# A hand-ordered attention and feed-forward kernel: the later part of the order rewritten, 24 half tiles masked by GpSimd

## The chip, the core and the metric

The kernel runs on one core of a Trainium2 chip. The core has five engines that run side by side, each through its own instructions in order: TensorE (PE, and PEld for its weight loads) multiplies matrices into PSUM, VectorE (DVE), ScalarE (ACT) and GpSimd (POOL) work element by element, and SyncE (SP) issues transfers. The metric is the time of one execution on the device in microseconds (us); smaller is better. The kernel before takes 441.9 us, the median of three runs from 441.88 to 443.86 us.

## The reference

Eight batches of eight heads, 576 positions, 64 elements a head. Scores within `tau` of their row's maximum are kept; the others get no weight. What the attention returns goes through a feed-forward layer whose hidden units are the largest of three products.

```python
scores = scale * np.matmul(q, k.transpose(0, 1, 3, 2))
thresh = np.max(scores, axis=-1, keepdims=True) - tau
scores = np.where(scores >= thresh, scores, -1000000000.0)
scores = scores - np.max(scores, axis=-1, keepdims=True)
attn = np.exp(scores)
attn = attn / (np.sum(attn, axis=-1, keepdims=True) + 1e-09)
attn_out = np.matmul(attn, v)                     # (8, 8, 576, 64)
x = attn_out.transpose(0, 2, 1, 3).reshape(8 * 576, 512)
h = np.maximum(np.maximum(x @ w1, x @ w2), x @ w3)  # 512 -> 768
out = h @ w_out                                   # 768 -> 512
```

## The kernel before

The work is cut into **half tiles**: the scores of 128 query rows of one head against all 576 keys, 128x576 numbers in fp32. There are 36 of them in a batch and 288 in all; two make a step, whose normalised weights are turned by one transposing transfer. A "quad" is four heads of one batch. The last batch goes through the feed-forward layer in two parts (`SPLIT`), the others in one.

One half tile passes these stages, each written as one letter of the order:

- `S`: TensorE multiplies queries and keys into a PSUM bank `sc` (`scores`). Queries and keys were transposed before (`T`), copied out of PSUM (`a` on ScalarE into `qt`, `c` on VectorE into `kt`), and GpSimd copied the query halves across into `qs` (`q`).
- `m`: VectorE reads `sc`, writes the scaled, negated scores to a buffer `z` (or to `stage`, which served the weights earlier) and leaves the row's extreme value in `nm`.
- Then the mask and the exponential, in one of several ways that a digit of the table `MASKED` sets for each half tile. Digit 0: VectorE makes a threshold `th` out of `nm` (`s`, 128x1), ScalarE flattens what is below it (`e`, a Prelu with a tiny slope) and takes the exponential with a row sum into `sm` (`n`). Digit 1: ScalarE takes the exponential at once with `nm` as its bias (`e`), and VectorE zeroes what is too small and sums up (`k`, a SCALAR_TENSOR_TENSOR with `z` as both inputs). Digits 2 and 3 are these two with ScalarE reading the scores straight from PSUM.
- `r`: VectorE takes the reciprocal of a step's two sums (`rs`), `p`: GpSimd multiplies each half by it and writes `P` in bf16, `t`: SyncE starts the transfer that turns `P` into `ptq`.
- `O`: TensorE multiplies `ptq` by the values, `w` (VectorE) and `x` (ScalarE) copy the result to `xt`.

The feed-forward layer of a batch follows as soon as its attention is done, in pieces `F` with a second half `B`: `ph` for the three hidden products (copied by ScalarE, `h`, into `hm`; combined on VectorE, `v`, into `hm` and then `hT`), `po` for the output (copied by ScalarE, `u`, and stored, `o`). The rest of the letters are loads (`l`, `g`), casts on GpSimd (`y`, `z`), the ninth chunk of rows (`N`, `j`, `i`) and the end (`f`, `d`).

Nothing decides the order at build time: the string `ORDER` is the program, letter by letter, and a digit behind `S`, `T`, `O`, `F` or `N` names one of four PSUM slots. Every engine is wrapped in `_Ordered`, which makes each instruction follow the one before it on the same engine, so the letters of one engine are its queue. All instructions carry the line of that wrapper, L93, in the profile; they are told apart by their tiles' names. PSUM has the four slots and no more: TensorE can't start a piece before the slot's last reader is done.

Of the kernel before, what the change touches and what calls it, by code (L numbers as in the profile page):

```python
# [11 lines left out]
F32 = mybir.dt.float32  # L12
# [23 lines left out]
PBUFS = 6  # L36

SPLIT = {7: ((0, 1), (2, 3, 4))}

ORDER = """  # L40
lllllllllT0laqqlcT1aS2lcqqgmS0S3lemS1lmnT2lmeS3lsaS0mnqlqemT3lyerclcapsnS1lS2eqmlS3qemznmS2perS1mnpsmnpT3ske
ytS1erkpT2agmnT3pclesqS2aqetS0meqlrnspmS1eqsT2nmpS3tnrcS0zlemS2eprmS3npmtS0npsgS1sermpS2emyS3eptmT0eplmS1ayl
meS0kynS2tssT3snkynkercperlT3pmnpmntqremS0lasprgeT3pmeS2psstnplnS0mzecesqrmS3etqkeS2gpnmS1npsmtnS0prmleS3pmS
2npsmnS0yrsmetperS2epmO1eqtnkplemnzswT2teS3rplS1empnmS3tpnssrS1klepS0mapermtS2epmT1S3nmqtnkO2qemncpS3txrskT1
peS2rmeS0ptmegpamS2npS1ertsmpnlkzS2elmS3eS0mpnlO1srkepsmnO2tyeprgwnpmT1xS3cpeS0sszmF2eS1meBqkF0ngqT3shrsmBay
S2tvpnF3rpemS1BpemF0pnsvT2BnyctS1esrlsT2mphS3lezS1maF0myntpT2sS3ngrcqF1eBmpnS2svpBnrmS3peS0tmeyF2zmnF3lBsvep
S0rhkBptesF2mgeS1zvF0nsmBpteBsrgvpnF1kS3phS2semBnqmF0S3evqF2ntrmBpelS1spvBnlmS3qhF0rsmepS1tnBpsmS3ezvS2eS1rm
pF0etsyO3mnlkngpO2eswetkBxrmpT3nF2rvpaS1BnqmS0hspS3meF2prS1smntBzesmF3ezvT0tBeclT1yS2pnvS0apsmtS3eyrmlS1epS2
mepF0mnqsmnS3tkBnkeF1restpkumeS2prtBumlperkpS0ustS2umS3pesmS1eqtT0mO2nlpceqsrmO3ntywelkS0pxlS1meF3prnS2smBye
myF0thpskS1oeBpF2nlvF3nlrmBpeBkpS1hstsvS0eF3lrmpnF2mBepBsveF1nT0vBtarkS3lhqS2smleF0prF1mnBysntBveS2plvnS0pom  # L50
F3nyS1pmeBsysmF0thT2rrlpeS1clF3epsmBnqT2svBaS1evqS2nmF0pS3nmqBtnmT2pS1hrcpS3esmS0petF2melS1rmpBnF3skpetF0sve
BlBmnF2vhtF1esrBkpnS0vtT3npBmS2arvpS0ermO3eqtsmepT1swntpS0cF2epesmtnS3kT1nS0mtBessrkpameS3preS1mS0uqmuS3mpnS
1tsmS2pnoS0rempS3lempO1lnkqlemO2lnymeO0srkpetkeF3swxykxpT2BercnprtS1uyS2upmF0termqS3eBymN2lhsskpelkS0eF3ertm
S1pjBlmeS0plvF2npS1mnyF3tpmnBsopT0nvBaS1kF2ieqrssmS0hlpBmelT1qF3snrvF0epcBlepS2vBnpsmtS1nS3rmphS2mnpF1smeS0B
snmF3tevS2T0mF1atBrsekpBevS0thS2pmF3nymS1qeBrsmnpS0tvF2eplF1rmnpBskeBptF3hsvS0eBrsstpmnS1lvT2qeO0mpnlscnT3wS
1etF2srramS0lnqBmlF3eqvT1nBcpS0thF2pemS1perS3mpBnmS0ptesO1smpnkteF3yvxT0BraktyS2esS1vpeS0mpnS3meqF2mnyrmpnT0
S1lceBqmeptrskS0pulS3muS1epmS2teF0rmplnskpeS1mtO3eklekO2esrmpesBknpwxS1kutS2urmopS3nF0myeS1mBetpsmF2hlS3rkep
BlmnF0S1prnsvT3tepBmF2apsssvS1eBtqmeS0qrS3hmtS1epsmF2lnpF0mleF3koBnBrvpeBstyvS1phsS2nmF3emS0nrS1tpmBnprS2smn
F0pveF1pBsremT3ptevBpS2chF0tnmF3ekBT1nvS2aBsmlnF0qvS1eS2rtrespmS3eBmqF1hmpT2nBcpS3ekpT2O0sasvterlmpO2ekqntwS
3xklpS1eF2ssmnF0yrBnmyS3evBptemS1plhS2ssmT3eyF0rcpeF1mBpntT3vnByS2ravpS0nmtpS3nsmS1eF2srmpektepS3slmnS0Bmeqn  # L60
mT1ktuS3urS0lcpeO2rlmpelmpeO3klpelweF1kqnsxS0rkepS2tmS3eBymemepS0kuF3quT2smeBtrF1kphoS0aBmnpS3tsN2rnvplnmpS1
erkpF0tjsF3mnBpsseBvS2ihrS1pmelS0mqeF3S2mnytBpmnoS1rF0eprsvF2ntpmBeBvqF1htskpS3esS0rmetS2pnmF3pBnmF0pesvT2te
BcF1nsBrvpntBskphT2F3erS0vlapBmnF1qvS2etpBmT0hS3rscpnF2lmS1qesS0sempBemS3yF1nvtS0nmBnT2ssrmpO3etspveF0wnS1rk
BpaS3tmhS2elqsF1mlS0qnmS3ermpBF2espsmS0npvBeS3tmeS1rvpO0ntmnsmS2yxS3empF0eskyerT1mpeS2cBtnypsmelkS3ulS2muS1e
smT0O3nsrplnpO2awetmeF3rkpxseT0S1ycntS2meF0poBrnsmpnkpF1ukBurS2shBqemF3oepvS0lS2nsmqF1emBptBnvF0hrrS2speS3mp
F1emBpntT2vepF3BssaktS0nvlBemS2hS1rsmptF0nS3mpeBmtnT2F1svnF3cetBBsrnvpS2hsrqS0meS1pmeT3F2sprmaS0npBmeF3ptsvn
S1qS0mnBtqmeS2yF1prevS0epssBmnS3qmS2htpmF0nlF1keBsmBertvO3pnvepF0serwpT2nBcpF3hktS1eBsrsmpnT0S2vtpaS1remqT3S
0nmyF2qectT1BpasmS3epvS1nS0mqnF2rmpemtpT3eS1keqS0smBercntpS1mupS3emF0ukessS1rmtpnBmopkS2uskS1eO3rukekO0yxeO3
ynwtprmopS0xmpS2emF3peS1mteBrsmpS0nF2pmhtS1nkBS3evF0nstmN2erkpeF1mBjpsBevS2hskF0eF3rkpteBmF1nBpveBkO2hsrvpeS
0rtwS1pnmF2npmS3eBympF1ntrvS0epBmpS2rF3svtpeS0mnpS1sBmiF2smhF0ntkBBervpS1etF3smpnF2BervpS1hsBpnmF0tevS3F1nmB  # L70
etrBkpO2vhO3nspS1xrwepS0mpF3smS2etF1snmBeBstvnS2S0veS3meF1snkeF2rmpnmpeBnkBerrptukpuO3rN1xpuO0jpuO3wptF1xpF2
hF0tvF1vF3hF0vtF1vF2hF0viF1vF2ohF0voF1vF3hF2vF1vF3hF2vO1vO0wF2xF3F1huF0vF3vF2ohF1vF3vF2hF0vF1vF3hF0vF2vF3hF1
vF2vF0hF1vF2vF0uF1ouN0ofjdi
# [31 lines left out]
def kernel(  # L105
# [684 lines left out]
    x = 0  # L790
# [39 lines left out]
```

## Time and profile before

| | |
|---|---|
| median of the runs | 441.9 us |
| span of the profiled execution | 440.2 us |
| PE busy | 418.9 us, 95% |
| PEld busy | 313.6 us, 71% |
| ACT busy | 403.6 us, 92% |
| DVE busy | 393.9 us, 89% |
| POOL busy | 317.0 us, 72% |
| mean granted TensorE clock | 0.988 |

The profile gives the profiled execution's time by its span, 440.2 us from the first to the last instruction; the runs' times are 1.7 us or more above it. In 40 slices of the span the page shows the busy tenths: TensorE is at 9 from the seventh slice or so to the last but one, VectorE and ScalarE drop in the last three, GpSimd in the last eight.

### The profile page before, as it was taken

How to read it: one execution, taken by the hardware profiler on the slowest of the kernel's cores; microseconds unless marked ns; L12 is line 12 of the kernel's file. 1: busy time of each engine (PE TensorE's matmuls, PEld its weight loads, DVE VectorE, ACT ScalarE, POOL GpSimd, SP SyncE). 2: the span in 40 equal slices, each digit the busy share in tenths (PEclk: the TensorE clock that was granted, in tenths of full speed). 3: DMA queues.
4: the chain of work that ended last, by engine and by line, in shares of the span. 5: the costliest groups of instructions: out<-in, count | busy, mean ns of one | idle time of the engine just before them, and what ended most of it. 6: DMA issues, size and time to landing. Idle time of an engine off the chain costs nothing.

```text
span 440.2 us, 14283 instructions
## 1 busy us (share of the span) xinstructions
PE 418.9 (95%) x5188; PEld 313.6 (71%) x5190; DVE 393.9 (89%) x1248; ACT 403.6 (92%) x834; POOL 317.0 (72%) x420
## 2 busy tenths in 40 slices
PE   7696789999999999999999999999999999999996
PEld 6353446787788776787678777887688777786873
DVE  4888899999999999999999999999889999998542
ACT  4999999999999999999999999999999998989521
POOL 1988999998787778867786778886585776554400
PEclk9987999999999999999999999999999999999999
DMA  6999999999999999999999999999698778583812
GB/s 190 276 239 214 270 215 260 263 252 252 220 277 224 237 165 242 291 160 232 189 242 238 202 182 273 192 199 208 135 237 153 147 109 185 102 169 72 192 50 85
DMA packets 213959, 88.50 MB, mean 201 GB/s; under 512 B 189184, under 2 KB 202240, under 8 KB 213888
## 3 DMA queue, kind: packets, MB, share of 16 engines
q1 hardware_dynamic: 213360, 86.96, 95.4%
q8 instruction: 41, 0.67, 0.6%
q10 hardware_dynamic: 528, 0.62, 0.5%
q14 instruction: 30, 0.25, 0.2%
HBM read 35.65 MB, written 9.44 MB: 102 GB/s over the span
## 4 chain that ended last, share of the span: by engine, by line
PE 78%; DVE 5%; POOL 5%; issue 4%; ACT 3%; DMA 2%; SPq 1%; DVEq 0%; POOLq 0%; ACTq 0%
PE ph L93 31%; PE sc L93 26%; PE po L93 10%; PE o L93 8%; POOL P L93 4%; PE tp L93 3%; ACT z L93 3%; DVE z L93 3%; DMA qm<-in_q_dram 2%; SPq L93 1%; DVE kt L93 1%; POOL w L93 1%; DVE stage L93 0%; DVE hm L93 0%; POOL qs L93 0%
## 5 line engine op out<-in xcount | busy, mean ns | idle before, releaser
L93 POOL TENSOR_SCALAR P<-z,rs 128x576 bf16<-128x576 f32 x250 | 202.0, 819 | 59.1 <-DVE rs L93 30.4
L93 DVE TENSOR_SCALAR_CACHE_REDUCE z<-sc 128x576 f32<-128x576 f32 x250 | 183.2, 749 | 12.2 <-PE sc L93 8.1
L93 PE MATMUL sc<-kt,qs 64*128 64x256 f32 (+2 forms) x640 | 179.8, 417 | 5.5 <-DVE z L93 3.9
L93 PE MATMUL sc<-kt,qt 64*128 64x320 f32 (+2 forms) x640 | 180.9, 429 | 3.1 <-DVE z L93 1.2
L93 PE MATMUL ph<-xt,w 64*128 64x288 bf16 (+2 forms) x2160 | 172.0, 283 | 0.2 <-DVE hm L93 0.2
L93 PEld LDWEIGHTS <-w 64*128 64x128 bf16 (+1 forms) x2160 | 128.0, 94 | 31.6 <-issue 4.0
L93 ACT ACTIVATE z<-z,th 128x576 f32<-128x576 f32 x161 | 120.5, 767 | 2.2 <-DVE th L93 1.9
L93 ACT ACTIVATE z<-z 128x576 f32<-128x576 f32 x175 | 117.6, 674 | 0.2
L93 PEld LDWEIGHTS sc<-kt,qs 64*128 64x128 f32 (+1 forms) x640 | 92.4, 179 | 22.5 <-DVE z L93 8.6
L93 PEld LDWEIGHTS sc<-kt,qt 64*128 64x128 f32 (+1 forms) x640 | 92.0, 179 | 14.7 <-DVE z L93 3.5
L93 DVE SCALAR_TENSOR_TENSOR z<-z 128x576 f32<-128x576 f32 x75 | 61.7, 827 | 1.4 <-ACT z L93 1.1
L93 POOL COPY qs<-qt 64x640 f32<-64x640 f32 (+3 forms) x66 | 45.9, 695 | 19.5 <-ACT qt L93 16.1
L93 ACT ACTIVATE z<-z,nm 128x576 f32<-128x576 f32 x72 | 53.9, 767 | 0.0
L93 PE MATMUL po<-wo,hT 64*128 64x512 bf16 (+3 forms) x454 | 53.3, 354 | 0.3
L93 DVE TENSOR_TENSOR hm<-ph,hm 128x576 bf16<-128x576 f32 (+2 forms) x54 | 37.0, 685 | 9.8 <-PE ph L93 9.6
L93 ACT ACTIVATE hm<-ph 128x576 bf16<-128x576 f32 (+2 forms) x54 | 31.9, 590 | 14.3 <-PE ph L93 13.8
L93 PEld LDWEIGHTS <-hT 64*128 64x128 bf16 (+2 forms) x456 | 28.4, 95 | 18.5 <-issue 2.6
L93 DVE TENSOR_TENSOR hT<-ph,hm 128x576 bf16<-128x576 f32 (+2 forms) x54 | 36.9, 683 | 2.8 <-PE ph L93 1.0
L93 PE MATMUL o<-ptq,vb 128*64 128x512 bf16 (+2 forms) x544 | 38.7, 282 | 0.2 <-DVE z L93 0.2
L93 POOL TENSOR_SCALAR P<-stage,rs 128x576 bf16<-128x576 f32 x38 | 29.5, 783 | 11.7 <-DVE rs L93 8.4
L93 ACT ACTIVATION_READ_ACCUMULATOR z<-z 128x1 f32 x175 | 33.6, 192 | 0.0
L93 PEld LDWEIGHTS <-vb 128*64 128x64 bf16 x544 | 22.4, 111 | 14.0 <-issue 5.6
(44 smaller groups left out, 412.2 us busy)
## 6 DMA issues: line engine op xcount, KB each, us to landing
vm<-in_v_dram SPq DMA_DIRECT2D x32, 256.0 KB, 4.6
qm<-in_q_dram SPq DMA_DIRECT2D x15, 512.0 KB, 4.7
km<-in_k_dram SPq DMA_DIRECT2D x15, 512.0 KB, 5.4
out_dram<-ob SPq DMA_DIRECT2D x14, 512.0 KB, 4.5
stage<-in_moe_w_dram SPq DMA_DIRECT2D x9, 512.0 KB, 5.6
ptq<-P SPq DMA_TRANSPOSE x144, 4.5
vr<-in_v_dram SPq DMA_DIRECT2D x16, 128.0 KB, 3.8
stage<-in_moe_w_out_dram SPq DMA_DIRECT2D x3, 512.0 KB, 5.5
```

Of the source, the lines that this page charges most:

```text
L93: ins = fn(*a, **kw)
```

## The change

The change has two parts. First, the table `MASKED` differs from the fourth batch on: digits 4 and 5 are new. Digit 0 stands 189 times instead of 187, digit 1 59 times instead of 84, digit 2 14 times as before, digit 3 once instead of three times, digit 4 24 times, digit 5 once. The 24 stand in batches four to eight: 3, 4, 5, 6 and 6. Second, the later part of `ORDER` is written anew. On each engine the instructions stand as before until the work of the third batch's feed-forward layer and of the fourth batch's scores; from there on they are in another order.

A half tile with digit 4 takes this way: `m` and `s` on VectorE as with digit 0; `b`, a first pass on GpSimd, that writes for each score one byte, the upper byte of a bf16 number in `far` (a huge number where the score is below the threshold, a zero otherwise); `C`, a second pass on GpSimd, that adds `far` to `z`; and `G`, one exponential on ScalarE with the bias `nm` and the row sum, in which the huge numbers become zero. There is one `far` buffer. Digit 5 has VectorE compare the scores in PSUM with the threshold instead of the exponentials.

The rest of the diff is small: `nm`, `th`, `sm` and `rs` of two half tiles share a tile, there are two `hm` buffers in place of three, `far` is cleared once at the start, and there are new functions behind switches that are off (`LOOSE`, `JOINED`, `BY_DMA`, `ONE_S`, `ONE_R`, `X_ON_DVE`, `U_ON_DVE`).

```diff
 MASKED = """
 220202110002002100110000100020020312000112012010100000000010100000001100
-001000111010000101100000000000110001100000011110110200100000100010000000
-110001101110100100010000001001100100000100101111102300000100100000001000
-001000110100100001000000000100100001011110100011011100002100001000001013
+001000111010000101100000000000110001100000011110110100040000100000400400
+100000100044210000400000001401100000000410001411101010420000010004000401
+040000100010040040400004000400001000001000115410004000404000400041200000
 """
...
 ORDER = """
...
-2npsmnS0yrsmetperS2epmO1eqtnkplemnzswT2teS3rplS1empnmS3tpnssrS1klepS0mapermtS2epmT1S3nmqtnkO2qemncpS3txrskT1
...
+S2vhS0pemF3tnbS1mF2nsrCsS0meBsmeF1pBvGpBeF3rvtbS0hpS2nmF1pnmBeCtBrsveS2F0npmS3GpBvF2ntsmF1hBkeS3svS0erBmnpO2
...
     def exponents(c, r):
         z = c["z", r]
         src, sign = (c[r], -1.0) if direct(c, r) else (z, 1.0)
+        if on_pool(c, r):
...
+                scalar.activation(out=z, in_=z, func=AF.Exp, bias=c["nm", r], scale=-1.0, accum_out=summed(c)[:, r:r + 1])
+            return
...
+    def marked(c, r):
+
+        c["far", r] = t = far[next(fars) % FARS]
+        pool.tensor_scalar(out=t.bitcast(mybir.dt.int8).rearrange("p (n x) -> p n x", x=2)[:, :, 1],
+                           in0=c["z", r], scalar1=c["th", r], scalar2=FAR, op0=OP.add, op1=OP.mult)
+
+    def moved(c, r):
+        pool.tensor_tensor(out=c["z", r], in0=c["z", r], in1=c["far", r], op=OP.add)
...
+        if by_mask[2 * number[c["g"], c["idx"]] + r] == "5":
+            vector.scalar_tensor_tensor(out=dst, in0=c[r], scalar=c["th", r], in1=z,
+                                        op0=OP.is_ge, op1=OP.mult, accum_out=acc)
...
-                    st["hm", f] = hp_.tile([128, nr, n], BF16, name="hm", bufs=3)
+                    st["hm", f] = hp_.tile([128, nr, n], BF16, name="hm", bufs=2)
...
+        elif what == "G":
+            exponents(*line["G"].pop(0))
+        elif what == "b":
+            c, r = line["b"].pop(0)
+            marked(c, r)
+            line["C"].append((c, r))
+        elif what == "C":
+            c, r = line["C"].pop(0)
+            moved(c, r)
+            line["G"].append((c, r))
```

Three places show how the instructions stand. The first is GpSimd's queue in the last batch; `P<-z,rs` is the normalisation, `vb` and `vr` are casts of values. Before:

```order
L93 TENSOR_SCALAR P<-z,rs 128x576 x4
L93 CAST vb<-vm 128x1024
L93 CAST vr_101<-vr 64x128
L93 TENSOR_SCALAR P<-z,rs 128x576 x3
L93 TENSOR_SCALAR P<-stage,rs 128x576 x2
L93 TENSOR_SCALAR P<-z,rs 128x576 x8
```

Now, with `far` written by the first pass and added by the second:

```order
L102 CAST vb<-vm 128x1024
L102 CAST vr_101<-vr 64x128 x2
L102 TENSOR_SCALAR P<-stage,rs 128x576 x2
L102 TENSOR_SCALAR P<-z,rs 128x576 x3
L102 TENSOR_SCALAR far_104<-z,th 128x576
L102 TENSOR_TENSOR z<-z,far_104 128x576
L102 TENSOR_SCALAR P<-z,rs 128x576 x4
L102 TENSOR_SCALAR far_104<-z,th 128x576
L102 TENSOR_TENSOR z<-z,far_104 128x576
L102 TENSOR_SCALAR P<-z,rs 128x576 x2
```

The two passes stand in the queue between the normalisations.

The second is VectorE's queue for the last half tiles before the end of the score work; `z,nm<-sc` is the maximum, `z,sm<-z` the mask. Before:

```order
L93 TENSOR_SCALAR z,nm<-sc 128x576
L93 TENSOR_SCALAR th<-nm 128x1
L93 SCALAR_TENSOR_TENSOR z,sm<-z 128x576
L93 RECIPROCAL rs<-sm 128x2
L93 TENSOR_SCALAR z,nm<-sc 128x576 x2
L93 SCALAR_TENSOR_TENSOR z,sm<-z 128x576
L93 RECIPROCAL rs<-sm 128x2 x2
L93 SCALAR_TENSOR_TENSOR z,sm<-z 128x576
L93 RECIPROCAL rs<-sm 128x2
```

Now:

```order
L102 TENSOR_SCALAR z,nm<-sc 128x576
L102 SCALAR_TENSOR_TENSOR z,sm<-z 128x576
L102 TENSOR_SCALAR th<-nm 128x1
L102 TENSOR_TENSOR hm<-ph,hm 128x576
L102 RECIPROCAL rs<-sm 128x2
L102 TENSOR_SCALAR z,nm<-sc 128x576 x2
L102 RECIPROCAL rs<-sm 128x2
L102 TENSOR_SCALAR th<-nm 128x1 x2
L102 RECIPROCAL rs<-sm 128x2
```

One mask stands where three stood, and there are more thresholds.

The third is ScalarE's queue in the last batch; `z<-z,th` flattens, `z,sm<-z` is the exponential with a sum, `z<-z,nm` the exponential with a bias. Before:

```order
L93 ACTIVATE z<-z,th 128x576
L93 ACTIVATE z,sm<-z 128x576
L93 ACTIVATE z<-z,nm 128x576 x2
L93 ACTIVATE ob_7967<-po 128x512
L93 ACTIVATE z<-z,nm 128x576
L93 ACTIVATE hm<-ph 128x576
L93 ACTIVATE stage<-stage,th 128x576 x2
```

Now, where `z,sm<-z,nm` is the exponential with both:

```order
L102 ACTIVATE z,sm<-z,nm 128x576
L102 ACTIVATE z<-z,th 128x576
L102 ACTIVATE hm<-ph 128x576
L102 ACTIVATE z,sm<-z 128x576
L102 ACTIVATE z<-z,th 128x576
L102 ACTIVATE z,sm<-z,nm 128x576
L102 ACTIVATE z,sm<-z 128x576
L102 ACTIVATE z<-z,th 128x576
```

Single passes with a bias have become single passes with a bias and a sum, and they stand behind the two passes on GpSimd.

At the end, after the last scores, TensorE's queue holds 8 matmuls of `ph`, 70 of `o` and then 60 of `po`, where it held 48 of `po`, 10 of `o`, 12 of `po` and 40 of `o`; what follows is alike in both.

More of the change, by code (lines that the diff above doesn't have):

```diff
@@ L46 @@
[L46 to L50, printed above, removed]
@@ L375, in threshold, with limited, together @@
     def threshold(c, r):
-        th = c["th", r] = small.tile([128, 1], F32, name="th", bufs=5)
-        vector.tensor_scalar(out=th, in0=c["nm", r], scalar1=-1.0, scalar2=tau, op0=OP.mult, op1=OP.subtract)
+        if "ths" not in c:
+            c["ths"] = small.tile([128, 2], F32, name="th", bufs=5)
+        mine = slice(0, 2) if together(c) else slice(r, r + 1)
+        for x in range(mine.start, mine.stop):
+            c["th", x] = c["ths"][:, x:x + 1]
+        vector.tensor_scalar(out=c["ths"][:, mine], in0=c["nms"][:, mine], scalar1=-1.0, scalar2=tau, op0=OP.mult, op1=OP.subtract)
+    def limited(c, r):
+        return by_mask[2 * number[c["g"], c["idx"]] + r] in "045"
+    def together(c):
+        return c["n"] >= ONE_S and limited(c, 0) and limited(c, 1)
     def exponents(c, r):
@@ L440, in first @@
                                   start=(m == 0), stop=(m == 4))
+            if joined and r == 0:
+                L["other"] = ps
+            elif joined:
+                for *q0, p0, n in runs:
+                    for i in range(2):
+                        for x, t in enumerate((L["other"], ps)):
+                            rows = slice(64 * x, 64 * x + 64)
+                            tensor.matmul(t[64 * i:64 * i + 64, p0:p0 + n], vrb[rows, 2 * x + i, :],
+                                          pt[rows, 4, q0[i]:q0[i] + n], start=False, stop=True)
         def on_vector():
@@ L641 @@
     number = {x: n for n, x in enumerate(steps)}
+    second = set()
+    for n in range(max(ONE_R, 0) + 1, len(steps)):
+        (g0, i0), (g1, i1) = steps[n - 1:n + 1]
+        if g0 == g1 and i0 != 4 and i1 != 4 and n - 1 not in second:
+            second.add(n)
     Ls, xts, stores, stores9, ends, ninths = {}, {}, [], [], [], []
```

223 lines of the change are left out of this document (155 added, 68 removed).

## The prediction

> **What bounds the kernel now.** I read the profile in this order: the chain of waits, busy time by stretch, the waits of TensorE, then the groups of instructions for prices. The chain first: four fifths of the span are TensorE work.
>
> ```profile
> PE 78%; DVE 5%; POOL 5%; issue 4%; ACT 3%; DMA 2%; SPq 1%; DVEq 0%; POOLq 0%; ACTq 0%
> ```
>
> That share says little before one knows where the rest lies. Followed in order of time, the chain leaves TensorE often in the first 80 us, while the first batch's softmax fills the pipe, and afterwards at two places only. These are pieces of it (start, length, what):
>
> ```profile
> 185.93 0.16 issue
> ...
> 341.00 0.97 PE sc L93 x8
> ...
> 356.41 0.49 DVE z L93
> ...
> 361.17 0.75 POOL P L93
> ...
> 375.29 0.83 PE po L93 x12
> ...
> 388.85 2.45 PE ph L93 x40
> ...
> 402.97 5.18 PE po L93 x48
> ...
> 431.87 4.41 PE po L93 x28
> ```
>
> From 186 to 189 us and from 356 to 375 us the chain runs over VectorE and GpSimd; everywhere else from 80 us to 436 us it is matmul after matmul. The two written orders agree, engine by engine, until about 163 us of this trace (eleven half tiles into the fourth batch's maxima on VectorE). So the stretch to look at is 163 us to the last scores at 403 us, and a tail that is TensorE's alone. Busy time of each engine there (PE, PEld, DVE, ACT, POOL, clock, DMA, GB/s):
>
> ```profile
> 163.00:403.00 240.00, 239.60 (x3174) 183.52 (x3174) 230.51 (x726) 233.32 (x477) 176.19 (x231) 1.00 0.96 193
> 163.00:351.00 188.00, 187.66 (x2504) 143.94 (x2504) 181.60 (x572) 185.55 (x381) 143.39 (x187) 1.00 1.03 208
> ```
>
> Of 240 us TensorE is busy 239.6, ScalarE 233.3 (97.2%), VectorE 230.5 (96.0%), GpSimd 176.2 (73.4%). Three engines are nearly full, and the clock is full, so no gift is to be had there. A busy TensorE may hide short stalls, since its ends are modelled; these would show at its weight loads, so I read their waits from 163 to 436 us (us in total, times, longest):
>
> ```profile
> PEld L93 <- issue: 9.2, 31, 0.4
> ...
> PEld tp L93 <- DVE z L93: 0.8, 3, 0.3
> ...
> PEld sc L93 <- ACT z L93: 0.7, 2, 0.4
> ...
> PEld tp L93 <- ACT ob L93: 0.2, 1, 0.2
> PEld sc L93 <- DVE stage L93: 0.2, 1, 0.2
> ```
>
> The 13 rows of that answer that name VectorE, from the 0.8 us for z to the 0.2 us for stage, come to 5.1 us; the 5 that name ScalarE, from z to ob, to 1.9 us; nothing waits longer than 0.4 us. The 9.2 us of "issue" wait for no engine. So TensorE is the bound, its matmuls stay the same in number and shape, and another order can win at most the 7.0 us of small waits. It can lose much more, as soon as one of the other three engines comes late.
>
> **The change part by part.** 87 half tiles were masked on VectorE by a SCALAR_TENSOR_TENSOR; now it is 61, one of them in a new form that reads the scores. 24 go over GpSimd in two passes and then one exponential with a sum on ScalarE. Prices (busy us, mean ns, idle before):
>
> ```profile
> L93 POOL TENSOR_SCALAR P<-z,rs 128x576 bf16<-128x576 f32 x250 | 202.0, 819 | 59.1 <-DVE rs L93 30.4 <-issue 5.6 <-DVE th L93 4.9
> ...
> L93 ACT ACTIVATE z<-z 128x576 f32<-128x576 f32 x175 | 117.6, 674 | 0.2
> ...
> L93 DVE SCALAR_TENSOR_TENSOR z<-z 128x576 f32<-128x576 f32 x75 | 61.7, 827 | 1.4 <-ACT z L93 1.1
> L93 ACT ACTIVATE z<-z,nm 128x576 f32<-128x576 f32 x72 | 53.9, 767 | 0.0
> ...
> L93 POOL TENSOR_SCALAR P<-stage,rs 128x576 bf16<-128x576 f32 x38 | 29.5, 783 | 11.7 <-DVE rs L93 8.4 <-ACT z L93 0.8 <-POOL vr L93 0.7
> ...
> L93 POOL CAST vb<-vm 128x1024 bf16<-128x1024 f32 x16 | 17.4, 1086 | 3.2 <-PE o L93 2.8
> ```
>
> Instructions overlap at their ends, so the price is the step from one start to the next (start, length):
>
> ```profile
> 388.57 0.15 DVE L93 TENSOR_SCALAR th<-nm 128x1 f32<-128x1 f32 x1
> 388.64 0.75 DVE L93 TENSOR_SCALAR_CACHE_REDUCE z<-sc 128x576 f32<-128x576 f32 x1
> ...
> 389.92 0.68 ACT L93 ACTIVATE z<-z 128x576 f32<-128x576 f32 x1
> 390.50 0.19 ACT L93 ACTIVATION_READ_ACCUMULATOR z<-z 128x1 f32 x1
> 390.59 1.43 ACT L93 ACTIVATE z<-z,th 128x576 f32<-128x576 f32 x2
> 391.92 0.67 ACT L93 ACTIVATE z<-z 128x576 f32<-128x576 f32 x1
> ```
>
> VectorE: a threshold steps 0.07 us, a mask 0.827 less the 0.07 overlap, 0.76 us. 26 masks fewer are -19.8 us, 27 thresholds more +1.9 us: -17.9 us. Its 230.5 us in the stretch become 212.6 us (88.6%).
>
> ScalarE: the exponential with its sum and the limiting pass before it step 0.67 us each. An exponential with a bias and a sum isn't in the trace: the bias adds 767 - 674 = 93 ns, so 0.76 us, 0.09 more than the 0.67 us which a masked half tile's single pass takes. 24 of these are +2.2 us; two half tiles more take the limiting pass and the exponential, which adds 2 x 0.67 = +1.3 us; two passes that no longer read the scores straight, +0.1 us. Sum +3.6 us: 233.3 becomes 236.9 us (98.7%), as full as ScalarE already is from 163 to 351 us (185.55 of 188).
>
> GpSimd: neither pass is in the trace. The first has one input as P<-z has, and the second reads two. How P runs alone and beside a mask is seen here:
>
> ```profile
> 251.39 0.74 DVE L93 SCALAR_TENSOR_TENSOR z<-z 128x576 f32<-128x576 f32 x1
> ...
> 251.46 1.28 POOL L93 TENSOR_SCALAR P<-z,rs 128x576 bf16<-128x576 f32 x1
> ...
> 254.18 1.46 POOL L93 TENSOR_SCALAR P<-z,rs 128x576 bf16<-128x576 f32 x2
> ```
>
> 0.73 us alone, 1.28 us beside a mask. First pass: 0.73 to 1.28 us, I take 0.75. Second: 0.73 (as one input) to 1.46 us (its two inputs read one after the other); it reads 1152 elements a partition, nearest to the cast of 1024 in 1.09 us, so 1.2. A pair is 1.95 us (1.46 to 2.74), 24 of them +47 us (35 to 66). Back comes what masks cost P: all 288 P over 0.73 us each are 202.0 + 29.5 - 210.2 = 21.3 us on 87 masks, 0.24 us each, and 26 fewer give 6.4 us. Net +40 us (28 to 59): 176.2 becomes 217 us, 90% of the stretch (85 to 98%).
>
> The Trainium skill (GPSIMD Engine Reference, Elementwise) warns against this very move: two-input work is about half as fast on GpSimd as on VectorE, 4497 ns for 2048 elements; an estimate for 576 is 1.26 us, by which a pair would be 2.0 us and the sum 1.5 us higher. The same page (Specifications) says that GpSimd shares its SBUF interfaces with VectorE's instructions of two SBUF inputs; the 1.28 us agree. What the trace can't show is whether the second pass in turn slows VectorE.
>
> What costs nothing rests on these rows (the first is the list of transfers, the others are the tail in time):
>
> ```profile
> ptq<-P SPq DMA_TRANSPOSE x144, 4.5
> ...
> 412.54 0.42 DVE L93 TENSOR_TENSOR hT<-ph,hm 128x256 bf16<-128x256 f32 x1
> ...
> 414.12 0.38 ACT L93 ACTIVATE hm<-ph 128x256 bf16<-128x256 f32 x1 [0.93 <-PE ph L93]
> ```
>
> It is two buffers for hm instead of three (even in the tail, where they follow each other fastest, the copy that takes up a buffer again starts at 414.12 us, over 1 us after VectorE has left it at 412.96 us), statistics of two half tiles in one small tile, one more memset before the first scores. After the last scores TensorE now finds 70 product matmuls ahead of the output projection's 48, where formerly the 48 came first and covered the last transposes. The fifth transpose these products need stands five half tiles earlier, some 7 us at the pace of 440.2 us for 288 half tiles; landing takes 4.5 us, so I take 0 (up to 3 us if it is late).
>
> **The sum.** TensorE's time doesn't change but for its waits. VectorE's idle time in the stretch goes from 9.5 to 27.4 us, almost threefold; I let the 5.1 us of waits for it fall to a third, -3.4 us. ScalarE's idle time halves, from 6.7 to 3.1 us; I let the 1.9 us of waits for it double, +1.9 us. Together -1.5 us on a span of 440.2 us. The runs' median, 441.9 us, lies 1.7 us above the span, and that rest stays: 441.9 - 1.5 = 440.4 us. About 0.5% (2.2 us) is what a measurement of this kernel can tell from no change, so this is no measurable change.
>
> **Rivals.**
>
> *GpSimd's queue becomes the bound (slower).* P stands in the same queue behind the two passes, and TensorE's products wait for P's transpose. For it: the order gives the last two batches 12 of the 24 pairs, and P already stands on the chain at 361 to 372 us. Against it: GpSimd mostly waits for others.
>
> ```profile
> POOL P L93 <- DVE rs L93: 38.8, 31, 5.0
> ```
>
> It decides from a pair price of (240 - 176.2 + 6.4) / 24 = 2.9 us, just over my upper bound of 2.74; at 3.2 us GpSimd needs 247 us, 7 us more than the stretch has: 441.9 + 7 = 449 us. With late P at the upper bound some 3 us are lost: 445 us.
>
> *ScalarE becomes the bound.* Of its 6.7 us of idle time it spends 4.1 waiting for TensorE:
>
> ```profile
> ACT hm L93 <- PE ph L93: 1.9, 7, 0.5
> ...
> ACT ob L93 <- PE po L93: 1.3, 3, 0.9
> ACT xt L93 <- PE o L93: 0.7, 2, 0.5
> ...
> ACT qt L93 <- PE tp L93: 0.2, 1, 0.2
> ```
>
> If these stay, 2.6 us are left for 3.6, and the stretch grows by 1.0: 442.9 us.
>
> *All waits on VectorE go, and ScalarE's don't grow (faster).* -5.1 us: 436.8 us; with ScalarE's too, 434.9 us. For it: VectorE loses as much work as it had idle twice over. Against it: 98.7% on ScalarE.
>
> **How the numbers follow.** Forecast 0.38 (438.5 to 442.3 us), faster rival 0.26 (434.9 to 439.6), ScalarE 0.16 (442 to 445), GpSimd 0.20 (444.2 to 450). Faster by over 0.5% (under 439.7 us): 0.26 and 0.12 of the forecast, 0.38. Slower (over 444.1 us): 0.20 and 0.03 of the ScalarE case, 0.23. The rest, 0.39, is within 0.5%. The range from 436.5 to 446.5 us leaves out about a tenth on either side; the forecast alone has 438.5 to 442.3.
>
> **What would show it.** Busy times of before stand in the page's first part:
>
> ```profile
> PE 418.9 (95%) x5188; PEld 313.6 (71%) x5190; DVE 393.9 (89%) x1248; ACT 403.6 (92%) x834; POOL 317.0 (72%) x420
> ```
>
> In the new profile VectorE should be busy near 376 us (393.9 less 17.9), ScalarE near 407, GpSimd near 357; a pair near 2 us; the chain still on TensorE after 189 us; waits of weight loads for VectorE under 2 us. Long waits of product matmuls for transposes, or P seldom waiting for rs, speak for the GpSimd rival; ScalarE at 99% with TensorE waiting for z for its own. I am wrong if the score work from 163 us on, 240 us long now, changes by more than 4 us, or if a pair costs over 2.74 us.

## The result, and the profile after

The kernel after takes 446.2 us, the median of 10 runs from 444.1 to 448.8, against 442.3 us for the kernel before beside it: a ratio of 1.0086 [1.0063, 1.0109], slower by a little under 1%. Taken once more it was 444.3 us against 441.7, a ratio of 1.0071 [1.0050, 1.0093]. I had forecast 440.4 us and no measurable change. The profiled execution took 444.59 us, with a span of 442.4 us, 2.2 us more than before.

The parts of the page after that answer to those shown of before: busy time, the chain, and the row of P with the idle time of GpSimd ahead of it.

```profile
PE 422.0 (95%) x5188; PEld 317.3 (72%) x5190; DVE 384.3 (87%) x1224; ACT 405.6 (92%) x862; POOL 361.2 (82%) x468
...
PE 84%; POOL 5%; ACT 4%; DVE 4%; issue 2%; POOLq 0%; DVEq 0%; ACTq 0%
...
L102 POOL TENSOR_SCALAR P<-z,rs 128x576 bf16<-128x576 f32 x250 | 194.4, 792 | 20.6 <-DVE rs L102 7.3
```

VectorE gave up 9.6 us over the span and GpSimd took 44 us more, its idle time ahead of P falling from 59.1 to 20.6 us. The chain holds more TensorE work than before, 84 in place of 78%. So no other engine has become the bound for long, and the time must be lost in small pieces. The busy time by stretch of the kernel after (columns as in the prediction) says the same:

```profile
163.00:403.00 240.00, 239.61 (x3146) 184.68 (x3146) 222.35 (x708) 235.55 (x503) 220.75 (x280) 1.00 0.94 193
```

ScalarE 98.1%, GpSimd 92.0%, VectorE 92.6%: close to the loads that were planned (98.7, 90 and 88.6%), but for VectorE, which gave up less. TensorE is called busy in both kernels, since its ends are modelled, yet it got less done. The waits of its weight loads, 163 to 436 us, those groups that name an engine:

```profile
PEld sc L102 <- DVE z L102: 2.0, 7, 0.5
PEld L102 <- PE ph L102: 1.1, 3, 0.4
...
PEld sc L102 <- ACT hm L102: 1.0, 3, 0.4
...
PEld tp L102 <- ACT hm L102: 0.6, 2, 0.4
```

All rows of that answer that name VectorE come to 3.9 us (5.1 before), those that name ScalarE to 2.4 (1.9 before), and rows that before did not have (a hidden piece or a score ahead, a pass of GpSimd, a transpose) to 2.1 us. Where VectorE waits, by its own waits from 163 to 403 us: first before, then after.

```profile
DVE z L93 <- PE sc L93: 2.4, 8, 0.6
```

```profile
DVE z L102 <- PE sc L102: 5.9, 13, 1.4
```

VectorE waits for scores more than twice as long as before, while scores still wait for VectorE's `z`: the row of 2.0 us above was, before,

```profile
PEld sc L93 <- DVE z L93: 0.8, 3, 0.3
```

The relief went into idle time of VectorE at other places than those where TensorE needed it.

Since busy shares can't show a loss of this kind, I read TensorE's progress: from the matmul records of two traces, the time at which each starts the same amount of matmul work. The table at the end of the experiments gives it. It takes the old order with the new code (e1 below) for its zero. By it the profiled execution of after is 1.0 us behind by 161 us, where the orders have hardly parted, and 2.6 us further behind at the end; that of before is 0.7 us behind by 161 us and 0.7 more at the end. The profiled execution of e1 was the fastest of its twelve, 441.06 us against a median of 441.74, so differences between rows say more than their size.

### The profile page after: what moved, and what is told of

It is laid out like the page before. It is cut to its first block, busy times and chain, and to the rows that moved or that the text cites. A ratio compares the mean times of both kernels' runs of the same rounds, so it can differ in the third digit from the quotient of the medians.

```text
span 442.4 us, 14262 instructions
## 1 busy us (share of the span) xinstructions
PE 422.0 (95%) x5188; PEld 317.3 (72%) x5190; DVE 384.3 (87%) x1224; ACT 405.6 (92%) x862; POOL 361.2 (82%) x468
## 3 DMA queue, kind: packets, MB, share of 16 engines
q1 hardware_dynamic: 213360, 86.96, 92.6%
## 4 chain that ended last, share of the span: by engine, by line
PE 84%; POOL 5%; ACT 4%; DVE 4%; issue 2%; POOLq 0%; DVEq 0%; ACTq 0%
PE ph L102 32%; PE sc L102 29%; PE po L102 11%; PE o L102 8%; PE tp L102 3%; ACT z L102 3%; POOL P L102 3%; DVE z L102 2%; POOL qs L102 1%; PE warm L102 1%; ACT qt L102 0%; POOL w L102 0%; DVE kt L102 0%; POOL vb L102 0%; DVE th L102 0%
## 5 line engine op out<-in xcount | busy, mean ns | idle before, releaser
L102 POOL TENSOR_SCALAR P<-z,rs 128x576 bf16<-128x576 f32 x250 | 194.4, 792 | 20.6 <-DVE rs L102 7.3
L102 PE MATMUL sc<-kt,qs 64*128 64x256 f32 (+2 forms) x640 | 181.7, 421 | 6.0 <-DVE z L102 4.0
L102 PE MATMUL sc<-kt,qt 64*128 64x320 f32 (+2 forms) x640 | 183.6, 433 | 2.8 <-ACT z L102 1.0
L102 PEld LDWEIGHTS sc<-kt,qt 64*128 64x128 f32 (+1 forms) x640 | 92.3, 179 | 15.7 <-DVE z L102 4.4
L102 ACT ACTIVATE z<-z,nm 128x576 f32<-128x576 f32 x74 | 56.3, 770 | 0.6 <-POOL z L102 0.5
L102 DVE SCALAR_TENSOR_TENSOR z<-z 128x576 f32<-128x576 f32 x53 | 45.9, 870 | 0.6 <-ACT z L102 0.6
L102 PE MATMUL o<-ptq,vb 128*64 128x64 bf16 (+2 forms) x544 | 38.5, 282 | 0.2 <-DVE z L102 0.2
```

Source lines behind the costliest of these rows:

```text
L102: ins = fn(*a, **kw)
```

## The experiments

Eighteen kernels in five groups. Unless another figure is given, a time is a median, and the kernel before beside it took 441.4 to 441.9 us. A ratio, with its interval in brackets, takes in all runs, so it isn't the quotient of the two medians.

**1. Which part of the change costs.** The kernel after once more; its code with the two tables of before; the new order without the passes; and the new order with the 24 masks back on VectorE.

```diff
 # e1: code of after
-MASKED, ORDER of after
+MASKED, ORDER of before
 # e4: order of after, 24 half tiles unmasked
-            marked(c, r)
-            moved(c, r)
 # e2: order of after
-digit 4 in MASKED; s, b, C, G
+digit 1; e where G stood, k just ahead of the half tile's r
```

> The changed kernel a second time, for a second profile and for how far its executions scatter: they lay between 444.1 and 448.8 us, before's between 441.7 and 443.9. If the loss is fixed in the order, the ratio is 1.005 to 1.011 again and the profile again shows TensorE some 2 us late at 342 us. If it hangs on when transfers land, executions scatter over 4 us again and another stretch of the profile loses.

> The changed program text with the order and the mask table of before: two buffers for hm, statistics of two half tiles in a tile, the cleared far buffer, and nothing else. Theory of the queue and theory of the order: 442.3 us, ratio 0.998 to 1.002. Theory of the small edits (a statistics tile or an hm buffer comes free later): ratio over 1.005.

> The changed kernel without the 48 passes on GpSimd; the 24 exponentials stand where they stood, so 24 half tiles keep scores below their threshold. GpSimd has some 50 us less to do and everything else the same place. Theory of the queue (P, its transposes and the z buffers come late behind the passes): back to 442.3 us or under it, ratio 0.990 to 1.002. Theory of the order (the positions of the new order cost the time, whoever masks): it stays at 445 us or more, ratio 1.006 to 1.010.

> The new order with the 24 half tiles masked by VectorE again, each mask written just ahead of its reciprocal, no pass and no threshold for them: GpSimd is relieved by 50 us, VectorE gets some 17 us more and is as full as before. Theory of the queue: faster than the changed kernel, 441 to 444 us. Theory of the order: 446 us or more, since VectorE now is full as well.

Measured: after 444.32 us; the new code in the old order 441.74, ratio 1.0007 [0.9993, 1.0021]; the new order without passes 443.03, ratio 1.0061 [1.0039, 1.0084]; with VectorE's masks 458.66, ratio 1.0386. The small edits cost nothing that these runs can tell. By the medians the positions alone cost about 1.3 us and the passes about 1.3 more. That split is rough: six of the ten runs without passes lie at 442.9 to 443.1 us and four at 445.7 to 447.2, so by means the positions cost 2.5 us and the passes 0.6. The traces, from 161 us on, put 1.4 us on the positions and 0.7 to 1.2 on the passes. The new order with its 24 masks back on VectorE is far slower: its stretch,

```profile
163.00:403.00 240.00, 231.65 (x2968) 171.69 (x2968) 225.11 (x688) 222.64 (x453) 167.01 (x223) 1.00 0.91 188
```

shows TensorE idle for over 8 us, and its weight loads wait most for VectorE (8.8 us for `z` in the same stretch). VectorE itself is busy for 225.1 of the 240 us, less than before, so it isn't simply full; what it does comes late where TensorE waits.

**2. What the relief is worth by itself.** In the order of before, 24 masks of the fourth to eighth batches simply dropped (f1); the same 24 with both passes put where the exponential stood, and the exponential where the mask stood (e3); the same without the passes (e3n).

```diff
 # f1: half tile by half tile, for 24 of them
-m ... e ... k
+m ... G            (G where e stood)
 # e3
-m ... e ... k
+m s ... b C ... G  (b C where e stood, G where k stood)
 # e3n: as e3
-            marked(c, r)
-            moved(c, r)
```

> The written order of before with 24 of VectorE's masks of batches 3 to 7 simply dropped (24 half tiles stay unmasked, that part of the computation is missing): their exponentials stay at their own place and make the sum as well (24 more sums of 0.19 us on ScalarE, 24 x 0.76 us less on VectorE). It measures what relief of VectorE is worth in the old order when nothing else moves. By the prediction's step that the rows waiting for VectorE fall to a third: 438 to 440.5. If the relief is worth nothing because the order was fitted to VectorE's pace or because ScalarE and TensorE set it: 441.4 to 442.3. If the 24 more sums on a ScalarE that is busy 97% of the time cost more than VectorE gives: 442.5 to 446.

> The written order of before, with 24 of its VectorE masks of batches 3 to 7 (one in every four or five) handed to GpSimd: the threshold follows the maximum, both passes stand where the exponential stood, exponential and sum stand where the mask stood; all else is the code of after. VectorE gives up about 24 x 0.76 = 18 us and gets 24 x 0.14 = 3.4 us back, GpSimd gets 24 x 2.05 = 49 us. Theory of the order (the loss of 1.3 us seen without any pass comes from the new positions, the passes cost little): 441.0 to 441.9, no slower than the old order. Theory of the queue (the two passes make P and the z buffers late wherever they stand): 443 or more. Theory that the masks were VectorE's only cost and that the old order simply never used the room: 439 to 440.5.

> As the old order with 24 pairs, but both passes are left out, so that 24 half tiles stay unmasked (that part of the computation is missing): the twin, in the old order, of the kernel that had the new order and no passes (443.03 us). Theory of the order: 440.5 to 441.7, at least 1.3 us under its twin, since the positions are all that differ. If instead VectorE's masks had been hiding nothing and their removal itself costs (ScalarE gets fuller by 24 sums), it comes out near its twin: 442.5 to 443.2.

Measured: f1 441.70 us, ratio 1.0004 [0.9987, 1.0021]. With VectorE free of 24 masks at no price to anyone but ScalarE's sums, nothing is won that these runs can tell. Its stretch, and the waits of its weight loads from 163 to 436 us that name VectorE, which come to 3.1 us in all (5.1 before); shown are two of the eleven:

```profile
163.00:403.00 240.00, 239.81 (x3182) 185.10 (x3182) 216.70 (x681) 235.18 (x502) 170.14 (x231) 1.00 0.95 194
```

```profile
PEld sc L111 <- DVE th L111: 0.5, 2, 0.2
...
PEld sc L111 <- DVE z L111: 0.2, 1, 0.2
```

Two of the five microseconds of waits are gone, and TensorE's progress from 161 us on is 0.6 us better. By this comparison these waits were worth about a third of their length; why, no run here shows. The runs can't tell these 0.6 us from nothing, and they lie within what the table repeats to at its end.

e3 took 465.95 us, ratio 1.0566, and e3n 448.36, ratio 1.0144. I had expected the old order with pairs to be as fast as the old order, and missed by 24 us. In e3 ScalarE stands still until a pass is done:

```profile
ACT z L113 <- POOL z L113: 9.7, 7, 2.4
```

In e3n no pass is left, and still 6.5 us are lost: all that differs from f1 is that 24 exponentials stand later in ScalarE's queue, and that 24 thresholds of 0.07 us came back. The waits of weight loads for `hm`, which only ScalarE's copy can set free, were not in the list of before; in e3n:

```profile
PEld sc L113 <- ACT hm L113: 2.7, 5, 1.2
```

That is less than half of the 6.5 us; where the rest is lost I did not take apart.

**3. What in the new order costs 1.3 us without passes.** Five kernels: three `hm` buffers instead of two; 24 half tiles without their sum; the 24 exponentials sooner; the new order up to 230 us only; and the two orders joined at 160 us both ways, where they hold the same pieces.

```diff
 # e5, from e4
-hp_.tile(..., name="hm", bufs=2)
+hp_.tile(..., name="hm", bufs=3)
 # f6, from e4
-            threshold(c, r)                               (for the 24)
-... bias=c["nm", r], scale=-1.0, accum_out=...)
+            vector.memset(summed(c)[:, r:r + 1], 1.0)
+... bias=c["nm", r], scale=-1.0)
 # g3, from e4: G where b stood
 # g4, from e4: ORDER of after to the 68th F, then what is left in the order of before
 # f4: the first 1104 pieces as in before, then as in after;  f5: the other way round
```

> The new order without the 48 passes (24 half tiles stay unmasked, that part of the computation is missing), and with three buffers for the copied hidden piece (hm) in place of two, as before had. The weight loads of the new order wait 1.2 to 1.6 us for hm where the old order named none. If the two buffers are what the new order stumbles over: 441.7 to 442.3, that is 0.8 to 1.3 us under the 443.03 of the same kernel with two. If the waits for hm only show a ScalarE that is late anyway: 442.8 to 443.2.

> The new order without the passes (443.03 us), and with the 24 exponentials of these half tiles not making their sum: VectorE writes a constant there instead, in the place of the threshold (24 half tiles unmasked and wrongly normalized: that part of the computation is missing). ScalarE gives up 24 x 0.19 = 4.6 us, VectorE's load is as before within 2 us. If the fuller ScalarE (235.6 of 240 us) is what the new order pays with: 441.5 to 442.3. If the loss comes from the positions on TensorE and the slots of scores only: 442.8 to 443.2.

> The new order without the passes (24 half tiles stay unmasked, that part of the computation is missing), with the 24 exponentials where the first pass stood, some ten pieces of the order earlier. If the room left for the passes is what makes the new positions dearer (it keeps z and the sums back): 441.7 to 442.4. If the other positions are the cause: 442.8 to 443.2, as with the exponentials in their late place.

> The new order, without its passes, up to about 230 us (the 172nd of 288 half tiles; the five or so half tiles handed over by then stay unmasked, that part of the computation is missing); from there the order and the masks of before. TensorE's progress in the profiles of the new order without passes fell behind by 0.5 us at 172 us, by 1.1 us at 204 to 236 us, and by 0.4 us more from 250 to 342 us. If the loss sits in the places themselves: 442.3 to 442.9, TensorE about 1.1 us behind the old order at 230 us and no further behind after it. If it is the relieved VectorE's new rhythm as a whole that costs: 441.7 to 442.2, or, if the old rest cannot take up from the new beginning, over 443.

> The kernel after, with the first 1104 pieces of the written order (to the 121st of 288 scores pieces, about 160 us) in the order of before; the two orders hold the same pieces up to there. If the loss and its scatter come from the rest (moved masks, ScalarE, GpSimd): 443.6 to 444.6, with single runs up to 448 as in after. If the scatter comes from the head (loads and transposes issued in another order, seen as a late q in one profile): 443.3 to 444.0 with all runs within 1 us.

> The counterpart: the first 1104 pieces in the new order, all that follows and all masks as before, no GpSimd pass. If the loss lies behind the head: 441.6 to 442.1, runs close together. If the head's new order brings lateness of the early loads: 442 to 444 with single runs 2 to 3 us above the others.

Measured: e5 443.63 us, f6 443.04, f4 444.73, f5 441.99. Three buffers and fewer sums give no time back, so neither the buffers nor ScalarE's sums are the cause. Nor is the beginning, or only for a small part: f5, with the new beginning alone, has a ratio of 1.0013 [1.0001, 1.0025], some 0.6 us, and its trace loses nothing behind 161 us. g3 took 449.72 us, where I had expected 441.7 to 443.2: bringing the exponentials forward costs 6.7 us, as much as putting them back did in the old order, and again the longest waits that name an engine are for ScalarE's copy:

```profile
PEld sc L113 <- ACT hm L113: 2.9, 5, 0.8
...
PEld tp L113 <- ACT hm L113: 1.4, 3, 0.7
```

g4 took 443.50 us. In its trace TensorE falls behind by 1.2 us between 161 and 203 us, just as in every other kernel with the new order there (1.2 to 1.3 us; 1.7 in one), stands 0.4 us further behind once the orders are joined, and loses nothing after it. Between two orders such figures hang on how a matmul is weighed. At 161 and at 207 us, though, the two orders have started exactly the same matmuls; between these points the kernels with the new order lose 1.0 to 1.1 us (1.5 in e7). So the loss sits in places. The waits of weight loads between 161 and 206 us, in the old order with the new code and then in the new order without passes, all that name an engine:

```profile
PEld L102 <- PE po L102: 0.3, 1, 0.3
...
PEld tp L102 <- DVE xt L102: 0.3, 1, 0.3
PEld sc L102 <- DVE kt L102: 0.2, 1, 0.2
PEld tp L102 <- DVE th L102: 0.2, 1, 0.2
```

```profile
PEld sc L102 <- DVE z L102: 1.1, 4, 0.3
...
PEld tp L102 <- ACT hm L102: 0.4, 1, 0.4
PEld L102 <- PE ph L102: 0.4, 1, 0.4
PEld L102 <- PE po L102: 0.3, 1, 0.3
```

1.0 us against 2.2: four scores wait for the slot that VectorE's maximum has not left yet, one transpose for ScalarE's copy, and one weight load for a hidden piece ahead of it on TensorE itself. One of the four, 0.3 us at 161 us, the old order has as well, just ahead of this stretch, so the difference is 0.9 us, against 1.0 to 1.1 us of progress lost. Here, unlike in f1, nearly the whole of the waits seems to be lost; that these waits are the cause is a matching of sums, and no kernel took one of them away. The rest of the positions' loss, some 0.2 us net behind 207 us, is made of gains and losses at many places; I did not take it apart.

**4. How the passes cost.** The second pass left out (e7); one second pass moved (g1); all moved (g2).

```diff
 # e7
-            moved(c, r)
 # g1, GpSimd's queue at the tenth pair; g2 likewise at all 24
 TENSOR_SCALAR far<-z,th
-TENSOR_SCALAR P<-stage,rs x2
-TENSOR_SCALAR P<-z,rs
 TENSOR_TENSOR z<-z,far
+TENSOR_SCALAR P<-stage,rs x2
+TENSOR_SCALAR P<-z,rs
```

> After without the second pass (the addition), so that 24 half tiles stay unmasked (that part of the computation is missing); GpSimd gives up 24 x 1.3 = 31 us of its 220 in 163 to 403 us. Between no pass (443.03) and both passes (444.32). If time lost goes with GpSimd's load alone: 443.4 to 443.6 (20 of 49 us are left). If it comes only where GpSimd is nearly full, or from the two-input addition beside VectorE's: 443.0 to 443.2. If one more stop in the chain from maximum to exponential is what costs: 443.8 to 444.3.

> The kernel after with one instruction moved: the second pass of the tenth pair (at 282 us in the profiles), which stood behind three P instructions on GpSimd, follows its first pass directly. Theory of the late pair: ScalarE's wait of 0.49 us there, VectorE's of 0.36 behind it and TensorE's of 0.52 behind that go; 0.5 us less than after, 443.2 to 443.9 as a median (after: 444.32 and 444.73 in the last two comparisons with the same order), and in the profile the wait for VectorE's z between 284 and 286 us is under 0.2 us. If the passes cost through GpSimd's load or through the memory port: as after, 444.2 to 444.8, with the wait still there.

> As the run with one pass moved, but for all 24 pairs: each second pass follows its first pass directly, ahead of the P instructions that stood between them. If late exponentials are the passes' whole cost: 442.8 to 443.6, near the new order without passes (443.03). If what is gained there is lost because P, and with it the transposes behind it, comes 1.3 us later at 12 or so places: 444 to 445.5.

From 161 us on, the traces of after and of the new order without passes keep step until 275 us but for some 0.2 us, and part by 0.56 us between 279 and 291 us. There the timeline of the second run of after (start, length) shows one chain over four engines:

```profile
278.40 1.28 POOL L102 TENSOR_SCALAR far<-z,th 128x576 int8<-128x576 f32 x1
279.77 1.47 POOL L102 TENSOR_SCALAR P<-stage,rs 128x576 bf16<-128x576 f32 x2
281.21 0.74 POOL L102 TENSOR_SCALAR P<-z,rs 128x576 bf16<-128x576 f32 x1
281.92 1.28 POOL L102 TENSOR_TENSOR z<-z,far 128x576 f32<-128x576 f32 x1
...
283.24 0.78 ACT L102 ACTIVATE z<-z,nm 128x576 f32<-128x576 f32 x1 [0.49 <-POOL z L102]
283.92 0.19 ACT L102 ACTIVATION_READ_ACCUMULATOR z<-z,nm 128x1 f32 x1
...
284.13 0.17 DVE L102 RECIPROCAL rs<-sm 128x2 f32<-128x2 f32 x1 [0.36 <-ACT z L102]
...
285.06 0.14 PEld L102 LDWEIGHTS sc<-kt,qt 64*64 64x64 f32 x2 [0.52 <-DVE z L102]
```

The second pass stands behind three P instructions and ends at 283.20 us. ScalarE's exponential waits for it, VectorE's reciprocal for the sum, VectorE's next maximum stands behind the reciprocal, and TensorE's next scores wait 0.52 us for the slot. It is the only wait of ScalarE for a pass that is listed from 163 to 403 us. With this one pass moved (g1) the wait at that place is

```profile
PEld sc L113 <- DVE z L113: 0.2, 1, 0.2
```

and TensorE's loss between 279 and 291 us falls from 0.56 to 0.33 us. It doesn't fall to nothing; in g1 one maximum waits 0.23 us for P to leave a half tile's buffer (`DVE stage <- POOL P`), which may be why. The medians, 444.15 us for g1, 443.88 for g2 and 444.33 for e7, don't part from after's 444.3. In the traces g2 ends no better than g1: moving the other 23 passes wins nothing. e7 has nothing of the loss at 284 us, so the second pass is needed for it; but its trace loses 0.4 us at 197 us, where the others don't. So of the passes' cost, 0.7 to 1.2 us of TensorE's progress and about 1.3 us of the medians, about a quarter of a microsecond is shown to be the late pair; the rest at that place is likely P, later because of the passes ahead of it.

**5. Why the runs of after lie 5 us apart.** Those of before lie within 3. Profiles were taken of a few of the longer executions, and all had lost it before 110 us: 2.7, 1.4 and 4.1 us in executions of 445.9, 444.6 and 447.4 us. In the longest (g2's), SyncE's queue and TensorE's weight loads:

```profile
69.46 2.20 SPq L113 DMA_DIRECT2D qm<-in_q_dram  x1
...
75.81 0.50 PEld L113 LDWEIGHTS tp<-identf,qm 64*128 64x128 f32 x8 [2.41 <-DMA qm<-in_q_dram]
```

In the second run of after the same issue took 0.54 us, and TensorE met the load in time:

```profile
67.91 0.54 SPq L102 DMA_DIRECT2D qm<-in_q_dram  x1
```

In the profile of before it issued at 68.39 us, and TensorE waited 0.73 us. The load has little slack in either kernel. So I issued it sooner, in both.

```diff
 # h1 from before, h2 from after: SyncE's queue
-DMA_TRANSPOSE ptq<-P x4
+DMA_TRANSPOSE ptq<-P x3
+DMA k<-in_k_dram
+DMA qm<-in_q_dram
+DMA_TRANSPOSE ptq<-P
 DMA stage<-in_moe_w_dram
 DMA_TRANSPOSE ptq<-P
-DMA k<-in_k_dram
-DMA qm<-in_q_dram
```

> The kernel before with two DMA issues moved on SyncE's queue: the loads of k's and q's part for the fifth group of heads go ahead of the fourth transpose in the row at 59 to 65 us, instead of behind it and one more (about 61 to 62 us in place of 67.4 and 68.4). Theory of the late q: the wait of 0.4 to 0.7 us at 73.9 us in the profile of before goes, 440.9 to 441.5 with nearly all runs within 0.7 us. If the spread comes from elsewhere: 441.4 to 441.9, some runs still 1 us and more above the rest. If the transposes that the loads now pass are what becomes late: 442 to 443.

> The kernel after with the same two issues moved by the same two transposes. Theory of the late q: 443.5 to 444.0 with nearly all runs within 0.7 us, so that the rest of the difference to before, 2.1 to 2.6 us, is what lies behind 110 us. If the spread comes from elsewhere: a median of 444.2 to 446, runs up to 447 and more.

Measured: 444.97 us for h1, ratio 1.0075 [1.0048, 1.0103], and 446.91 for h2; the runs spread as much as before (443.9 to 448.3 for h1). The wait for q is gone, and a product of attention stops instead after two of its matmuls; in h1:

```profile
65.64 1.65 SPq L93 DMA_TRANSPOSE ptq<-P  x1
...
70.43 0.85 PEld L93 LDWEIGHTS <-vb 128*64 128x64 bf16 x14 [2.49 <-issue]
```

The trace names nothing for this wait; the transpose that the loads had passed was issued at 65.64 us, and transposes land in 5.1 us there (median), at 70.7 us by that. So it is probably the transpose: loads and transposes both arrive just in time there, one behind the other in one queue, and what is moved ahead makes the other late. Whether the new order makes executions run into this more often stays open. In the old order the runs spread over 3.5 and 3.8 us in twelve (e1, f1), and f5's over 3.3 in twelve; in the new order e4's spread over 4.3 in ten, and f4's over 1.5 in only five.

**TensorE's progress**, worked out from the matmul records: microseconds behind the old order with the new code (e1), with what was lost by 161 us taken off and shown by itself. The columns are five amounts of matmul work, named by e1's time. In the rows with another order than e1's, the columns before the last hang on how a matmul is weighed, and can be off by some 0.3 us or more; down a column, between rows of one order, they compare well.

```
                              by 161 |  203   235   289   342   434 us
before                           0.7 |  0.3   0.3   0.3   0.3   0.7
f5 new head, old rest            0.5 |  0.0   0.0   0.1   0.1   0.1
f1 old order, masks dropped      0.7 |  0.0  -0.3  -0.5  -0.5  -0.6
f6 no passes, no sums            0.5 |  1.2   0.9   1.0   1.6   1.2
e4 no passes                     0.1 |  1.2   0.9   1.1   1.8   1.4
e5 no passes, three hm           0.8 |  1.2   0.9   1.1   1.9   1.9
g4 new order to 230 us           0.4 |  1.2   1.0   1.6   1.6   1.6
g1 one pass sooner               1.4 |  1.2   1.1   1.6   2.3   1.9
g2 all passes sooner             4.1 |  1.3   1.1   1.6   2.3   1.9
a2 after again                   0.4 |  1.2   1.1   1.8   2.5   2.1
f4 old head, new rest            0.4 |  1.2   1.2   1.9   2.6   2.2
e7 first pass only               2.7 |  1.7   1.4   1.5   2.2   2.3
after                            1.0 |  1.3   1.2   1.9   2.6   2.6
e3n old order, late exponentials 0.1 |  0.8   1.5   2.8   4.2   6.3
g3 new order, early exponentials 0.4 |  2.5   3.0   4.3   6.0   7.9
```

The rows of before and f5, whose order from 161 us on is e1's, show how well the table repeats: 0.3 us up to 342 us, 0.7 at the end.

## Why the prediction was wrong

**The step that failed is the sum.** "I let the 5.1 us of waits for it fall to a third, -3.4 us", and ScalarE's double, +1.9 us. It was a guess from idle shares, made without asking where the idle time would come to lie. Measured: the rows naming VectorE fell from 5.1 to 3.9 us, those naming ScalarE rose from 1.9 to 2.4, and 2.1 us came in rows that the sum had no term for. Two errors stand behind it:

- A microsecond of a weight load's wait isn't a microsecond of TensorE's loss. Dropping 24 masks outright (f1) took 2.0 us off these waits and gave TensorE 0.6 us, and the runs nothing. So in the old order the relief of VectorE was worth 0 to 0.6 us, where the sum had 3.4.
- The new positions were costed at nothing, apart from the tail. I took it that a written order costs only through what it adds to engines. e4 shows that the new places cost 1.3 us by the medians with no pass and fewer masks, 1.0 to 1.1 of them between 161 and 207 us; e3n and g3 show by their 6.5 and 6.7 us how tight such an order is. ScalarE was busy 97% of the stretch before, and its queue is in order, so a copy that comes a little later holds a slot of TensorE's: in e3n such waits come to 2.7 us, in g3 to 4.3.

**Prices.** ScalarE came out at 405.6 us over the span (forecast 407), GpSimd at 361.2 (357). VectorE came out at 384.3 us, not near 376. By the groups' durations the masks gave 19.1 us, their read-outs 2.2, and the thresholds took 4.2, nearly as counted. But all its durations together fell by 15.7 us (478.9 to 463.2), and busy time by only 9.6, since the instructions overlapped by 6.1 us less (85.0 to 78.9). The step from start to start, by which I had priced, leaves that out. The passes, of which no row existed, by tile (minimum, median, maximum in ns):

```profile
L102 POOL TENSOR_SCALAR far<-z,th x22: 749/752/1299, 180.8 to 392.1; 128x576 int8<-128x576 f32 x22
L102 POOL TENSOR_TENSOR z<-z,far x22: 1278/1283/1722, 181.7 to 392.9; 128x576 f32<-128x576 f32 x22
```

0.75 and 1.28 us, 2.03 in the median and 2.2 in the mean, for 0.75 and 1.2 forecast. The Trainium skill (GPSIMD Engine Reference, Elementwise) gave the second better than my own row did: the estimate of 1.26 us from its 2048 elements agrees with 1.28. Of the sharing of SBUF that the Trainium skill speaks of (GPSIMD Engine Reference, Specifications), the other side can now be seen too, masks slowed beside GpSimd: in a2's trace, from 163 us on, ten masks that ran beside none of its instructions for over 0.2 us took 0.79 us in the mean, twelve beside a P 0.99, eight beside a first pass 0.84, and two beside a second pass 1.05; the passes go up to 1.30 and 1.72 us. The masks take 915 ns with the passes (a2) and 853 without (e4), but that this comes of the passes isn't shown, since most met a P or the shorter pass. Over 26 masks it is 1.6 us on VectorE, which had 18 us idle; no run here shows that it cost time.

**Edits costed at nothing cost nothing that the runs can tell**: e1, 1.0007, holds for the buffers, the shared small tiles and the memset. The product matmuls ahead of the output projection follow each other without a break from 403.78 us on in after's trace, as forecast.

**The rivals.** GpSimd's queue: the mechanism is there, at one place and for half a microsecond, not for the 3 to 7 us that I priced; P seldom waits for rs any more, which I had named as its sign, and yet it is no bound. ScalarE: its load isn't the cause (f6, without 24 sums, is as slow), while the places of its instructions can cost more than the whole loss (e3n, g3), which I had not separated. One row of this rival I had read from a stretch that runs to 410 us: from 163 to 403 us ScalarE waits 0.5 us for `o`, not 0.7, which makes 3.9 us in place of 4.1 and its time 442.7 us. All waits on VectorE go: f1 comes nearest to that rival, its waits for VectorE fall to 3.1 us, and it doesn't win.

**The signs and the range.** Waits of weight loads for VectorE, which I had put under 2 us, came to 3.9. Neither sign of being wrong appeared: a pair took 2.03 us, not over 2.74, and the loss from 161 us on was 2.6 us at most, not 4; both were too coarse for a loss of this size. The 446.2 us lie just inside the range that I gave, in the part that was there for the GpSimd rival, whose mechanism was seen at one place only. That the range holds them is luck.

**The time itself.** Against e1's, 2.1 to 2.6 us of TensorE's progress are lost behind 161 us and 0.4 to 1.0 before it in the two profiled executions of after. The first comparison's 446.2 us is more than these make; profiles of other executions show losses up to 4.1 us in the first 110 us, and I take the rest to be of that kind, which its own unprofiled runs can't show. No kernel here beats before: f1, which leaves work out, ties with it, so handing over such masks has nothing to win in the old order as it is written.

## What to carry to other kernels

When TensorE and a copying engine are both above 97%, ask of each piece that moves which slot it frees and who takes that slot next; busy time taken off a third engine is worth, in the order as written, what dropping it outright wins, and that is the first experiment to make. Compare progress at equal work, not busy shares: a pipelined TensorE is called 99.8% busy in a kernel that loses 2 us. Before moving a load forward in a shared queue, look at what it passes.

## What the runs showed that I had not expected

The same DMA issue on SyncE took 0.54 us in one execution and 2.20 in another, where TensorE then waited 2.41 us for the load. Writing every second byte (the first pass) cost GpSimd hardly more than writing bf16: 0.75 us for 576 elements, where P alone takes 0.73. And moving 24 exponentials, 18 us of ScalarE's work, by about 20 letters of the written order, three or four pieces of ScalarE's own queue, cost 6.5 to 6.7 us in either direction.
